# One K load of a decode attention kernel, cut into transfers of 112, 6, 6 and 4 partitions

## Chip, cores and metric

The kernel runs on one core of one Trainium2 chip. The metric is device time in microseconds (us) of one execution; lower is better. The times stated are medians over runs; beside them there is one profiled execution, from which the views are taken.

## The reference

A decode step for 4 sequences: layer norm, attention over a K/V cache of 32 heads and 4096 positions, a projection with a residual, then a layer norm and a small dense block with the mish activation and a second residual. Cut to what matters:

```python
# x (4,1,640), k_cache and v_cache (4,32,4096,128), wq (640,4096), wo (4096,640), all bf16
q = layernorm(x) @ wq                               # (4, 32 heads, 1, 128)
scores = einsum("bhqd,bhkd->bhqk", q, k_cache) * 128**-0.5
p = softmax(scores)
o = einsum("bhqk,bhkd->bhqd", p, v_cache)
h = x + o.reshape(4, 1, 4096) @ wo
y = layernorm(h) @ w1 + b1                          # w1 (640,1728)
act = y * tanh(softplus(y))
out = h + act @ w2                                  # w2 (1728,640)
```

Nearly all the bytes are the two caches: 4 x 32 x 4096 x 128 bf16 values each, 134 MB for K and 134 MB for V.

## The kernel before

**Groups.** The 4 x 32 pairs of sequence and head are worked in 32 groups (`NG = HQ * N`, 8 x 4). Group g belongs to one sequence b and G = 4 heads. Its K tile `kt` and its V tile `vt` have the shape [128, 128, 128]: 32 partitions to a head, 128 positions on each partition, 128 values to a position. So each partition holds 32 KB, which lie together in memory, and a load is 4 MB. `load_kv` (L88 to L97) issues it from the SP queue as one transfer of 128 partitions (L96). Only the last group's loads are made of two transfers, each of half the positions of all partitions (`np_`).

**Buffers and the order of loads.** There are two K buffers and two V buffers (`KBUFS`, `VBUFS`). The order is written out by hand in the loop over g: when group g's scores are done, K of group g+2 is issued into the buffer of group g; then V of group g+1. SP issues in this order, and before each it waits until the buffer's old content has been used: for K by VectorE and TensorE, for V by TensorE. The names K28, V27 and so on stand below for the loads of those groups. From K28 on the order is K28, V27, K29, V28, K30, V29, K31 (two transfers), V30, V31 (two), then w1, the rest of w2 (`w2s` of 128 and `w2r` of 64 partitions) and three parts of w2. Earlier loads are x (4 partitions, from the ACT queue), wq, four parts of wo and b1 (one partition).

**Work on a group.** `mul_and_sum` takes half a tile at a time (`part`): VectorE (DVE) multiplies K by the broadcast q in place (L337, two instructions to a part), and TensorE (PE) sums over d by matmuls with the identity (L344). `finish_sum` (L356) ends the sum on VectorE, `softmax` finds the maximum of each head through a transpose (L367 to L382) and takes the exponential on ScalarE (L387). `pv_moving` (L245) multiplies the weights by V for the group before; `add_blocks` (L259) folds its four blocks. The last two groups' products with V are taken by `pv` (L271) after the loop. Then come the projection (L318), the second layer norm, and the dense block (L514, L576), and one store of 20 partitions (L600).

On TensorE the order is that of the program: the sums of group g's second part stand before the V product of group g-1, and that before the sums of group g+1.

Of the kernel before, what the change touches and what calls it, by code (L numbers as in the profile page):

```python
# [16 lines left out]
def kernel(  # L17
# [23 lines left out]
    nc = tc.nc  # L41
# [4 lines left out]
    N = B * Sq  # L46
# [7 lines left out]
    HQ = H // G  # L54
# [4 lines left out]
    WOC = 8  # L59
    NQ = 2  # L60
    DQ = Dh // NQ
    KBUFS = 2
    VBUFS = 2
    NE2 = 2
# [12 lines left out]
    pad.tile([128, 192], BF16, name="pad")  # L77
    kpool = ctx.enter_context(tc.tile_pool(name="kpool", bufs=KBUFS))
    vpool = ctx.enter_context(tc.tile_pool(name="vpool", bufs=VBUFS))
# [8 lines left out]
    def load_kv(pool, tag, cache, g):  # L88
        hq, b = divmod(g, N)
        t = pool.tile([128, R, Dh], BF16, tag=tag, name=f"{tag}{g}")  # L90
        view = cache[b, G * hq : G * (hq + 1)].rearrange("h (p r) d -> (h p) r d", p=PH)

        np_ = NP if g == NG - 1 else 1
        for i in range(np_):
            r0, r1 = i * R // np_, (i + 1) * R // np_
            nc.sync.dma_start(out=t[:, r0:r1, :], in_=view[:, r0:r1, :])  # L96
        return t  # L97

    def load_k(g):
        return load_kv(kpool, "kt", A_k_cache, g)  # L100

    def load_v(g):
        return load_kv(vpool, "vt", A_v_cache, g)
# [35 lines left out]
    for q in range(G):  # L139
        nc.vector.tensor_copy(  # L140
            out=sel[:, :, q, q * PH : (q + 1) * PH],
            in_=ident[0:N, 0:N].unsqueeze(2).to_broadcast([N, N, PH]),
# [185 lines left out]
    def mul_and_sum(g, part):  # L328
# [6 lines left out]
        for k in range(NQ):  # L335
            d0 = k * DQ
            nc.vector.tensor_tensor(  # L337
                out=kt[:, :, d0 : d0 + DQ],
                in0=kt[:, :, d0 : d0 + DQ],
                in1=qbs[:, hq, b, d0 : d0 + DQ].unsqueeze(1).to_broadcast([128, RP, DQ]),  # L340
                op=ALU.mult,
            )
            for d in range(d0, d0 + DQ, W):
                nc.tensor.matmul(  # L344
# [52 lines left out]
    for g in range(NG):  # L397
# [31 lines left out]
        if g in WO_AT:  # L429

            if not wo_sb:
# [3 lines left out]
                out=wo_sb[0][:, h0 : h0 + WOC, :],  # L435
                in_=A_wo.rearrange("(h p) n -> p h n", p=128)[:, h0 : h0 + WOC, :],
# [60 lines left out]
    for dst in (h2T, hc):  # L497
        nc.vector.tensor_tensor(
            out=dst[:, :, :],
# [11 lines left out]
    for c in range(FC):  # L511
# [9 lines left out]
        if c == 4:  # L521
# [3 lines left out]
                out=std[:, :], in_=v_ps[:, :], func=ACT.Sqrt, bias=eps_t[:, :], scale=1.0  # L525
# [5 lines left out]
        out=h1n[:, :, :],  # L531
# [6 lines left out]
        out=h1s[:, :, :],  # L538
# [9 lines left out]
        out=tb[:, :, :],  # L548
# [8 lines left out]
        out=ta[:, :, :], in0=tb[:, :, :], scalar1=-0.5, scalar2=-1.0, op0=ALU.mult, op1=ALU.add  # L557
# [4 lines left out]
        out=act_t[:, :, :],  # L562
# [10 lines left out]
    for i, (w2, c) in enumerate(w2_of):  # L573
# [11 lines left out]
        out=oT[:, :, :].rearrange("p n c -> p c n"),  # L585
# [46 lines left out]
```

## Time and profile before

| what | value |
|---|---|
| time, median of 3 runs | 671.55 us (671.48 to 672.41) |
| time of the profiled execution | 672.24 us |
| its span (first to last instruction) | 670.4 us |
| PE busy | 562.8 us (84%) |
| DVE busy | 351.6 us (52%) |
| ACT busy | 112.2 us (17%) |
| DMA: bytes, mean rate over the span | 283.81 MB, 423 GB/s |
| queue q1 (all loads issued by SP): share of the 16 DMA engines' time | 98.6% |
| DVE's waits for K loads | 211.6 us in 30 waits |
| K load: issue to landing, median | 23.8 us |

The span is what the profile's views cover; what lies outside it (1.84 us here) is the difference to the profiled execution's time. The busy shares are means over the span. "Idle before, releaser" in a view is the time in which an engine stood still just before an instruction, and what ended it. A line `SPq` is SP's DMA queue; the time from issue to landing of a load contains its time in the queue behind the loads ahead of it. The profile's DMA line gives the busy share of all 16 DMA engines in tenths, in 40 slices of the span. Besides the views the trace holds a record of each DMA packet: start, duration, size and queue.

### The profile page before, as it was taken

What the parts mean: (1) busy time and instruction counts of PE and PEld (TensorE: products, weight loads), DVE (VectorE), ACT (ScalarE), POOL (GpSimd) and SP (SyncE); (2) the same over time, 40 slices, a digit from 0 to 9 for tenths busy, and PEclk for the clock granted to TensorE, in tenths of its full rate; (3) what the DMA queues carried; (4) which work ended last, traced back from release to release, by engine and by line L of the source; (5) the groups of instructions that cost most, each with busy time, mean ns of one, the idle gap of its engine ahead of it and who ended that gap; (6) DMA issues with size and microseconds to landing.
All of it is one profiled execution on the core that took longest, in us unless ns stands there. A gap on an engine that the chain in (4) does not pass through costs nothing.

```text
span 670.4 us, 7163 instructions
## 1 busy us (share of the span) xinstructions
PE 562.8 (84%) x3121; PEld 255.9 (38%) x3121; DVE 351.6 (52%) x304; ACT 112.2 (17%) x343; POOL 2.4 (0%) x13
## 2 busy tenths in 40 slices
PE   0589999799998886688998899869987899888985
PEld 0234444344443342233443344333433344333454
DVE  2385455455654456336664444666543566644642
ACT  0021121221220111011110111111101111110131
POOL 1000000000000000000000000000000000000000
PEclk9999999899997997878999899898999799997995
DMA  9999999999999999999999999999999999999994
GB/s 374 438 437 436 427 429 427 437 436 435 429 428 427 428 425 428 430 428 430 431 437 436 431 431 425 436 434 435 431 434 425 436 435 432 435 429 428 434 414 175
DMA packets 15191, 283.81 MB, mean 423 GB/s; under 512 B 1267, under 2 KB 5559, under 8 KB 6584
## 3 DMA queue, kind: packets, MB, share of 16 engines
q1 hardware_dynamic: 15152, 283.36, 98.6%
q8 instruction: 24, 0.39, 0.2%
q14 instruction: 7, 0.06, 0.0%
q10 hardware_dynamic: 8, 0.01, 0.0%
HBM read 283.35 MB, written 0.01 MB: 423 GB/s over the span
## 4 chain that ended last, share of the span: by engine, by line
PE 45%; DMA 34%; DVE 19%; issue 1%; ACT 1%; SPq 0%; DVEq 0%
DMA kt<-in_A_k_cache_dram 34%; PE s L344 21%; DVE kt L337 16%; PE p L245 15%; PE ot L259 3%; PE q_ps L191 1%; PE qb_ps L205 1%; PE ot L271 1%; PE tr L369 1%; DVE mx L374 1%; DVE s_sb L356 1%; ACT q_all L198 1%; PE l_ps L283 0%; PE h_ps L514 0%; PE yT L318 0%
## 5 line engine op out<-in xcount | busy, mean ns | idle before, releaser
L337 DVE TENSOR_TENSOR kt<-kt,qbs 128x4096 bf16<-128x4096 bf16 x128 | 291.4, 2279 | 211.6 <-DMA kt<-in_A_k_cache_dram 211.6
L344 PE MATMUL s<-kt,ident 128*128 128x512 bf16 x1024 | 262.9, 404 | 77.1 <-DVE kt L337 77.0
L245 PE MATMUL p<-vt,e 128*16 128x512 bf16 x960 | 215.8, 384 | 0.0
L344 PEld LDWEIGHTS <-ident 128*128 128x128 bf16 x1024 | 99.2, 102 | 197.5 <-issue 97.2
L245 PEld LDWEIGHTS <-e 128*16 128x16 bf16 x960 | 84.7, 91 | 131.0 <-issue 20.2
L387 ACT ACTIVATE e<-s_sb,nbs 32x128 bf16<-32x128 f32 x128 | 73.9, 577 | 2.5
L253 ACT COPY p_sb<-p 16x512 f32<-16x512 f32 x30 | 17.2, 574 | 317.9 <-PE p L245 317.9
L356 DVE TENSOR_REDUCE s_sb<-s 128x64 f32<-128x512 f32 x64 | 43.4, 679 | 3.8 <-PE s L344 3.7
L374 DVE TENSOR_REDUCE mx<-tr 1x4 f32<-1x128 f32 x32 | 8.9, 277 | 50.0 <-PE tr L369 49.8
L384 ACT COPY nbs<-tr 128x4 f32<-128x4 f32 x32 | 5.2, 162 | 173.0 <-PE tr L382 173.0
L259 PEld LDWEIGHTS ot<-ident_f,p_sb 16*128 16x128 f32 x240 | 28.9, 186 | 12.7 <-issue 12.7
L387 ACT ACTIVATION_READ_ACCUMULATOR e<-s_sb,nbs 32x1 f32 x128 | 32.1, 251 | 0.0
L259 PE MATMUL ot<-ident_f,p_sb 16*128 16x4 f32 x240 | 31.5, 250 | 0.0
L191 PE MATMUL q_ps<-wq_sb,xT 128*4 128x512 bf16 x40 | 11.0, 409 | 9.8 <-DMA wq_sb<-in_A_wq_dram 9.8
L382 PEld LDWEIGHTS tr<-mx,nscale 1*128 1x128 f32 x64 | 9.4, 183 | 13.8 <-issue 13.1
L291 DVE RECIPROCAL rl<-l_ps 128x16 f32<-128x16 f32 x8 | 2.1, 257 | 23.0 <-PE l_ps L283 23.0
L369 PE MATMUL tr<-ident_f,pm 128*1 128x128 f32 x64 | 12.9, 285 | 1.2 <-DVE pm L367 1.2
L205 PE MATMUL qb_ps<-q_all,sel 4*128 4x128 bf16 x128 | 9.2, 225 | 5.3 <-ACT q_all L198 5.3
L382 PE MATMUL tr<-mx,nscale 1*128 1x4 f32 x64 | 12.2, 258 | 0.4 <-DVE mx L374 0.4
L205 PEld LDWEIGHTS <-sel 4*128 4x128 bf16 x128 | 8.4, 98 | 9.1 <-issue 9.1
L198 ACT CAST q_all<-q_ps 4x512 bf16<-4x512 f32 x8 | 4.6, 574 | 35.4 <-PE q_ps L191 35.4
L367 DVE TENSOR_REDUCE pm<-s_sb 128x1 f32<-128x128 f32 x32 | 9.2, 286 | 1.1
(79 smaller groups left out, 75.1 us busy)
## 6 DMA issues: line engine op xcount, KB each, us to landing
kt<-in_A_k_cache_dram SPq DMA_DIRECT2D x31, 4096.0 KB, 23.8
vt<-in_A_v_cache_dram SPq DMA_DIRECT2D x31, 4096.0 KB, 26.5
wq_sb<-in_A_wq_dram SPq DMA_DIRECT2D x1, 5120.0 KB, 15.4
wo_sb<-in_A_wo_dram SPq DMA_DIRECT2D x4, 1280.0 KB, 29.0
kt<-in_A_k_cache_dram SPq DMA_DIRECT2D x2, 2048.0 KB, 19.0
vt<-in_A_v_cache_dram SPq DMA_DIRECT2D x2, 2048.0 KB
w<-in_B_w_dram SPq DMA_DIRECT2D x1, 2160.0 KB, 21.2
w<-in_B_w_dram SPq DMA_DIRECT2D x3, 640.0 KB, 19.5
```

Of the source, the lines that this page charges most:

```text
L191: nc.tensor.matmul(q_ps[:, :], lhsT=xT[:, c, :], rhs=wq_sb[:, c, n * QC : (n + 1) * QC], start=(c == 0), stop=(c == DC - 1),)
L205: nc.tensor.matmul(qb_ps[:, b * Dh : (b + 1) * Dh], lhsT=sel[:, b, q, :], rhs=q_all[:, h * Dh : (h + 1) * Dh], start=(q == 0), stop=(q == ...
L245: nc.tensor.matmul(p_ps[:, :], lhsT=e2[g % NE2][:, r : r + J, :].rearrange("p j q -> p (j q)"), rhs=vt[:, r : r + J, :].rearrange("p j d - ...
L253: nc.scalar.copy(out=blocks[g][:, :], in_=p_ps[:, :])
L259: nc.tensor.matmul(o, lhsT=p_sb[:, j * Dh : (j + 1) * Dh], rhs=ident_f[0 : J * G, j * G : (j + 1) * G], start=(j == 0), stop=(j == J - 1),)
L337: nc.vector.tensor_tensor(out=kt[:, :, d0 : d0 + DQ], in0=kt[:, :, d0 : d0 + DQ], in1=qbs[:, hq, b, d0 : d0 + DQ].unsqueeze(1).to_broadcas ...
L344: nc.tensor.matmul(s_ps[:, :, :], lhsT=ident[:, :], rhs=kt[:, :, d : d + W], start=(d == 0), stop=(d == Dh - W),)
L356: nc.vector.tensor_reduce(out=s_sbs[g][:, part * RP : (part + 1) * RP], in_=s_of.pop((g, part))[:, :, :], axis=AX.X, op=ALU.add,)
L369: nc.tensor.matmul(tr_ps[0:1, 0:128], lhsT=pm[:, :], rhs=ident_f[:, :], start=True, stop=True)
L374: nc.vector.tensor_reduce(out=mx[:, :], in_=tr_ps[0:1, 0:128].rearrange("o (a b) -> o a b", a=G), axis=AX.X, op=ALU.max,)
L382: nc.tensor.matmul(nb_ps, lhsT=nscale[:, :], rhs=mx[:, :], start=True, stop=True)
L387: nc.scalar.activation(out=e2[g % NE2][p0:p1, :, q], in_=s_sb[p0:p1, :], func=ACT.Exp, bias=nb[p0:p1, q : q + 1], scale=SCALE, accum_out=r ...
```

## The change

`load_kv` makes the K load of one group, number N * HQ - 4 = 28 of 0 to 31, out of four transfers instead of one: partitions 0 to 111, 112 to 117, 118 to 123, and 124 to 127. All four are issued in a row from the SP queue, at the place where the one was issued. The bytes, the tile and everything else are the same; every other load stays one transfer of 128 partitions.

```diff
     DQ = Dh // NQ
+    FEW = ("kt", N * HQ - 4)
     KBUFS = 2
...
         np_ = NP if g == NG - 1 else 1
+
+        cuts = (0, 112, 118, 124, 128) if (tag, g) == FEW else (0, 128)
         for i in range(np_):
             r0, r1 = i * R // np_, (i + 1) * R // np_
-            nc.sync.dma_start(out=t[:, r0:r1, :], in_=view[:, r0:r1, :])
+            for p0, p1 in zip(cuts, cuts[1:]):
+                nc.sync.dma_start(out=t[p0:p1, r0:r1, :], in_=view[p0:p1, r0:r1, :])
         return t
```

## The prediction

> **What bounds the kernel now.** I read the page first, slices and queues, then the waits, the chain of the last 110 us, the timelines of SP and DVE there, and last the packet records. The page says that the 16 DMA engines never rest:
>
> ```profile
> DMA  9999999999999999999999999999999999999994
> GB/s 374 438 437 436 427 429 427 437 436 435 429 428 427 428 425 428 430 428 430 431 437 436 431 431 425 436 434 435 431 434 425 436 435 432 435 429 428 434 414 175
> q1 hardware_dynamic: 15152, 283.36, 98.6%
> q8 instruction: 24, 0.39, 0.2%
> ```
>
> Queue q1 (the loads) fills 98.6% of the engines' time, at some 432 GB/s. Engines this busy leave one thing to gain or lose: how evenly work lies on them. The waits name who pays:
>
> ```profile
> DVE kt L337 <- DMA kt<-in_A_k_cache_dram: 211.6, 30, 19.3
> ```
>
> VectorE's multiply by q waits 30 times for a K load. In DVE's timeline the first multiplies of groups 28, 29 and 30 read:
>
> ```profile
> 574.91 2.29 DVE L337 TENSOR_TENSOR kt<-kt,qbs 128x4096 bf16<-128x4096 bf16 x1 [8.22 <-DMA kt<-in_A_k_cache_dram]
> 594.23 2.29 DVE L337 TENSOR_TENSOR kt<-kt,qbs 128x4096 bf16<-128x4096 bf16 x1 [8.72 <-DMA kt<-in_A_k_cache_dram]
> 613.89 2.29 DVE L337 TENSOR_TENSOR kt<-kt,qbs 128x4096 bf16<-128x4096 bf16 x1 [5.92 <-DMA kt<-in_A_k_cache_dram]
> ```
>
> And the chain that ended last:
>
> ```profile
> 568.68 25.53 DMA kt<-in_A_k_cache_dram
> 594.23 2.29 DVE kt L337
> ...
> 608.03 3.57 PE s L344 x8
> 611.60 7.91 PE p L245 x32
> 619.52 1.83 PE s L344 x8
> ```
>
> Its last DMA is the K load of group 29 (K29), issued at 568.68 and landed at 594.23. From there on it is DVE and PE up to the output. K30 lands at 613.89 while PE is busy with p until 619.52: not on the path. So whatever moves **the last byte of K29** moves the end one for one. The altered load, K28, is two loads ahead of it (K28, V27, K29).
>
> **The streams in the packet records.** The trace holds start, duration, size and queue of each packet, not its engine. Where one packet's start meets another's end, they can be chained, and the loads form 16 streams without gaps: eight packets of 32 KB, 1.213 us each, and a semaphore packet per 4 MB load, so 9.68 us a load. 32 KB in 1.213 us is 27.0 GB/s, times 16 is the 432 of the page. (These records run 10.8 us ahead of the engines' clock: K29's last packet ends at 605.07, DVE starts at 594.23.) What sets streams apart is q8: eight of them carry its 24 packets (0.88 to 1.19 us) in turn; each costs its stream some 1.4 us, which it never wins back. At K29 the eight stand 2.85, 2.92, 3.05, 3.20, 3.21, 4.34, 4.37 and 4.51 us behind the earliest stream; the other eight 0, 0.13, 0.39, 0.44, 0.75, 1.06, 1.21, 1.54. K29 waits for the 4.51.
>
> **The change, part by part.**
>
> Issue: three more transfers on SP at 551.77. Two in a row took 0.80 (K31), so 3 x 0.40 = 1.2 us. The SP timeline shows them covered:
>
> ```profile
> 551.77 0.33 SPq L96 DMA_DIRECT2D kt<-in_A_k_cache_dram  x1
> 558.77 0.33 SPq L96 DMA_DIRECT2D vt<-in_A_v_cache_dram  x1
> 568.68 0.33 SPq L96 DMA_DIRECT2D kt<-in_A_k_cache_dram  x1
> ```
>
> V27 is issued 7.0 us later, after a wait for PE, and its packets start some 11 us after that. Cost 0; if that cover were gone, 1.2 us on V27, which lands at 584.6, 2.8 us before PE's p for it begins (587.4). DVE waits for four semaphores where it waited for one, and 3 x 9 ns of semaphore packets are added. K30's issue also names them, but it waits for K28 to be used up anyway: 0.
>
> Which stream gets which rows: in this trace 128 rows go eight to a stream, w2r's 64 rows four, the output's 20 rows as two packets each with ten semaphore packets, x's 4 rows as four, b1's one row as one. The count of streams is the largest up to 16 that divides the rows. So 112 becomes seven rows on all 16, and 6, 6, 4 become one row on six, six and four streams. Whether they begin at the same stream, the trace cannot say; I take it that they do. Then four streams have 10 rows, two have 9, ten have 7.
>
> In stream time alone: 7 rows instead of 8 are -1.21 us, 10 are +2.42. If late streams are among the ten, the 4.51 becomes 3.30. Two signs say so: b1's single row went down the stream at 0.44, and a row of x that took 755 ns ended 3 ns ahead of wq's first row on the stream now at 1.06. Both are among the eight without q8. The latter, as one of the four, becomes 1.06 + 2.42 = 3.48, and the worst of its kind 1.54 + 2.42 = 3.96. K29 would move by -1.03 to -0.55.
>
> The other half is **where the 16 rows land**. In a full load each stream writes eight partitions of its own, so the trace does not tell whether 27.0 GB/s is what a stream gives or what its partitions take. The 16 rows all go to partitions 112 to 127, and up to six streams write next to each other at once. Bounds: below, no sharing, one row per transfer, 3 x 1.21 = 3.63 us for streams 2 and 3 of the six. Above, all 16 rows through one 27.0 GB/s door, 16 x 1.21 = 19.4 us. Between: doors of four partitions. Then 112-115, 120-123 and 124-127 each pass four rows of different streams, 4 x 1.21 = 4.84 us, and streams 2 and 3 are in all three: 14.5 us. The nearest rows are w2r's, 64 partitions from 16 streams: 55 ns for 1280 bytes in 44 of 64 packets, up to 84 in the rest, where w2s (128 partitions, same size) stays at 55 in 117 of 128. That is contention, up to 84/55, in a burst of only 5 KB per stream; for 32 KB rows it says little. I take the doors of four, the least sharing in which 27.0 GB/s belongs to partitions, since a rate that is the same to 1 ns in 7881 of 7936 packets looks like a fixed door and not a shared memory.
>
> The Trainium skill's page "SBUF — State Buffer", section "Door 1: The DMA port swizzle", speaks against the change: 16 ports of about 27 GB/s each serve two groups of four partitions, and a transfer to four partitions is put at 27.6 GB/s in all, one to 64 at 196. By that page 112-115, 116-119, 120-123 and 124-127 are four ports, shared with the streams already writing V27 there; my estimate by it is +9 us. No row here shows 32 KB writes to one group.
>
> Sum: streams 2 and 3 need 7 x 1.21 + 14.5 = 23.0 us for K28 where they needed 9.68: +13.3. They start between 0 and 1.54 where the last stood at 4.51, so K29's last byte moves by 13.3 - 4.51 + (0 to 1.54) = +8.8 to +10.3. I take +8.8, as streams that finish early leave the door to others. K28 itself is later by as much: its 8.22 us of waiting grows, its 10.6 us of work (574.91 to 585.51 on DVE) still ends before K29 lands. Against the profiled execution (span 670.4, time 672.24, so 1.84 outside the span) that is 681.0; against the median of the runs, 671.55, which is 0.69 lower, **680.4**.
>
> **Rivals.**
>
> No shared door, early streams take the rows: K29 moves by -0.55 to -1.03, at most one row, -1.21. Time 670.3 to 671.0, say 670.8. For it: streams never disturb each other in 32 KB rows, and both signs on b1 and x. Against: they never had to share partitions. It decides if four streams into four partitions pass 32 KB in under 1.6 us each: 7 x 1.21 + 3 x 1.6 is 13.3, plus 1.06, just above 9.68 + 4.51. This is the case that ends not slower; by 0.18% at most, so hardly over the bound of 0.2% (1.34 us), about what a measurement of this kernel can tell from no change.
>
> No shared door, but the rows fall on streams with q8: 2.85 + 2.42 to 4.51 + 2.42, so +0.8 to +2.4, time 672.3 to 674.0. Against it the two signs above.
>
> The change does not load any stream more: the small transfers begin on streams in rotation, or each row is cut over all 16. Each stream has eight rows as before: 671.5, if there is no door; +3.6 (4.84 - 1.21) if there is.
>
> A door half as tight (two streams' worth) belongs to the forecast's own side: 8.47 + 3 x 2.42 + 1.06 - 14.2 = +2.6, 674.1. The widest sharing gives 13.3 + 4.9 - 4.51 + (0 to 1.54) = +13.7 to +15.2, 685 to 687.
>
> **How the numbers follow.** Shared door 0.68; no door and early streams 0.20; no door and late streams 0.06; no load shifted 0.06. Slower by over 0.2%: 0.68 + 0.05 of the late streams + 0.01 = 0.74. Faster by over 0.2% needs the whole row and some luck: 0.08 (a cause unseen included). The rest, 0.18, is within. The second case has 0.20, so the range reaches down to it, 670.3; up to 684.0, which leaves out the widest sharing, about 0.1. The forecast's own range is 674.1 to 687.
>
> **What would show it.** Right: the 128-row K packets keep 1.213 us, but the 16 packets of the small transfers take 4 us or more; DVE's wait ahead of group 28 grows from 8.22 to about 17 us and that ahead of 29 stays near 8.7; K29's landing moves from 594.2 to about 603; the chain behind it keeps its 74 us. Wrong: the small packets take 1.21 us (no door), DVE starts on group 29 before 594.2, or the 16 packets lie on 16 streams.

## The result, and the profile after

The change takes **688.23 us** (median of 5 runs, 687.93 to 689.42) against 671.55 of the kernel before on the same chip: a ratio of 1.0247, 95% interval 1.0235 to 1.026, or +16.7 us. The forecast was 680.4 with a range of 670.3 to 684.0. The direction held and the size did not: the loss is nearly twice the +8.8 us that were worked out. The profiled execution after has a span of 686.4 us, 16.0 more than before.

The page of the profile after, first the DMA rows (busy tenths and GB/s in 40 slices of 17.16 us) and the shares of two queues:

```profile
DMA  9999999999999999999999999999999999999994
GB/s 382 441 427 428 427 434 442 432 429 430 431 429 436 428 421 432 417 438 438 431 429 431 427 435 436 435 429 432 429 436 437 432 368 201 315 434 432 437 408 184
q1 hardware_dynamic: 15168, 283.36, 98.7%
q8 instruction: 24, 0.39, 0.2%
```

The busy row is the one of before, nines throughout, and q1's share is still 98.7%. The GB/s row is not: three neighbouring slices read 368, 201 and 315 where 432 is the normal pace. Against 432 they miss 64 + 231 + 117 = 412 GB/s for 17.16 us, 7.07 MB, and at 432 GB/s that is 16.4 us. The whole loss stands in these three numbers. The engines read as busy all the while, with transfers that went at less than their pace.

The waits, and the first multiplies of groups 28, 29 and 30 in VectorE's timeline (start, duration, operation, idle time before it and what ended it; L341 is the L337 of before):

```profile
DVE kt L341 <- DMA kt<-in_A_k_cache_dram: 223.1, 30, 25.7
```

```profile
591.86 2.29 DVE L341 TENSOR_TENSOR kt<-kt,qbs 128x4096 bf16<-128x4096 bf16 x1 [25.73 <-DMA kt<-in_A_k_cache_dram]
610.85 2.29 DVE L341 TENSOR_TENSOR kt<-kt,qbs 128x4096 bf16<-128x4096 bf16 x1 [7.76 <-DMA kt<-in_A_k_cache_dram]
630.17 2.29 DVE L341 TENSOR_TENSOR kt<-kt,qbs 128x4096 bf16<-128x4096 bf16 x1 [5.58 <-DMA kt<-in_A_k_cache_dram]
```

K28's wait went from 8.22 to 25.73 us, those of K29 and K30 hardly moved (8.72 to 7.76, 5.92 to 5.58). K28 is ready 16.95 us later than before, K29 16.62 us later. The loss arises while K28 is under way and is passed on, with nothing added or won back. The chain that ended last goes over K29 as before:

```profile
568.11 42.71 DMA kt<-in_A_k_cache_dram
610.85 2.29 DVE kt L341
...
653.27 22.56 DMA w<-in_B_w_dram
```

K29 is issued at 568.11, 0.6 us earlier than before, and takes 42.71 us instead of 25.53. Behind it the chain now passes over w1's load, but is no longer for it: 686.4 - 610.85 = 75.6 us, where before it was 76.2. SP's timeline shows what the additional issues cost:

```profile
551.20 1.37 SPq L100 DMA_DIRECT2D kt<-in_A_k_cache_dram  x4
558.21 0.35 SPq L100 DMA_DIRECT2D vt<-in_A_v_cache_dram  x1
568.11 0.35 SPq L100 DMA_DIRECT2D kt<-in_A_k_cache_dram  x1
```

Four issues take 1.37 us and are over 5.6 us before V27's.

**The packet records.** The normal 32-KB row takes 1.213 us. The records (on their clock, which runs 10.8 us ahead of the engines') hold 26 32-KB rows over 1.3 us before, each beside a packet of an instruction queue (q8 or q14), and 216 after. 191 of these stand in one stretch, from 571 to 603. Chained into 16 streams, as in the prediction, they divide so:

| rows | how long each took (us) | time over 1.21 us a row, summed, divided by 16 streams |
|---|---|---|
| 21 rows of V26, ahead | up to 2.53 | 1.3 us |
| the 112-partition transfer, seven rows on each of 16 streams | median 2.40 | 9.0 us |
| the 16 rows of the three small transfers | 2.6 to 3.7, medians 3.10, 3.29, 3.38 | 2.0 us |
| 42 rows of V27, behind | up to 3.66 | 3.9 us |
| sum | | 16.2 us, beside a span longer by 16.0 us |

All 16 streams are slow, not the four or six that carry small rows, and rows of the neighbouring whole loads are slow with them.

### The profile page after: what moved, and what is told of

It is laid out like the page before. It is cut to its first block, busy times and chain, and to the rows that moved or that the text cites. A ratio compares the mean times of both kernels' runs of the same rounds, so it can differ in the third digit from the quotient of the medians.

```text
span 686.4 us, 7172 instructions
## 1 busy us (share of the span) xinstructions
PE 563.1 (82%) x3121; PEld 256.2 (37%) x3121; DVE 351.5 (51%) x304; ACT 112.2 (16%) x343; POOL 2.4 (0%) x13
## 3 DMA queue, kind: packets, MB, share of 16 engines
q1 hardware_dynamic: 15168, 283.36, 98.7%
## 4 chain that ended last, share of the span: by engine, by line
PE 42%; DMA 39%; DVE 17%; ACT 1%; issue 1%; SPq 0%; DVEq 0%
DMA kt<-in_A_k_cache_dram 36%; PE s L348 20%; DVE kt L341 15%; PE p L249 15%; DMA w<-in_B_w_dram 3%; PE ot L263 3%; PE q_ps L195 1%; PE qb_ps L209 1%; PE tr L373 1%; DVE mx L378 1%; DVE s_sb L360 1%; ACT q_all L202 1%; PE h_ps L518 0%; PE l_ps L287 0%; PE y2T L580 0%
## 5 line engine op out<-in xcount | busy, mean ns | idle before, releaser
L341 DVE TENSOR_TENSOR kt<-kt,qbs 128x4096 bf16<-128x4096 bf16 x128 | 291.5, 2279 | 223.1 <-DMA kt<-in_A_k_cache_dram 223.1
L257 ACT COPY p_sb<-p 16x512 f32<-16x512 f32 x30 | 17.2, 574 | 320.0 <-PE p L249 320.0
L386 PEld LDWEIGHTS tr<-mx,nscale 1*128 1x128 f32 x64 | 9.4, 183 | 13.8 <-issue 13.1
```

The lines of the kernel that those rows point to most:

```text
L257: nc.scalar.copy(out=blocks[g][:, :], in_=p_ps[:, :])
L341: nc.vector.tensor_tensor(out=kt[:, :, d0 : d0 + DQ], in0=kt[:, :, d0 : d0 + DQ], in1=qbs[:, hq, b, d0 : d0 + DQ].unsqueeze(1).to_broadcas ...
L386: nc.tensor.matmul(nb_ps, lhsT=nscale[:, :], rhs=mx[:, :], start=True, stop=True)
```

## The experiments

Three theories stand in the expectations. A "door" in them is whatever passes the writes of the DMA engines into a group of neighbouring partitions; it is a name for a guess, and no record shows one. **A**: streams that write to partitions behind a common door share its pace, and this slows all 16 streams. **B**, the prediction's: only the streams that carry rows into a shared door are slowed, the rest runs on. **C**: it is the reading side, the addresses that a cut load reads, and the partitions have no part in it. Ratios are to the kernel before in runs of the same chip; the spans are those of one profiled execution each (before: 670.4).

### Only one cut: 112 and 16 partitions

```diff
-        cuts = (0, 112, 118, 124, 128) if (tag, g) == FEW else (0, 128)
+        cuts = (0, 112, 128) if (tag, g) == FEW else (0, 128)
```

> K28 in two transfers, of 112 and of 16 partitions: seven rows and then one row on each of the 16 streams, so no stream carries more bytes than before. Known from the run of the change: during the 112 every row on every stream took about 2.4 us instead of 1.21. Theory A (streams that write neighbouring partitions share a door, and all 16 streams go at the pace of the fullest door): 7 x 1.2 = +8.4 us for the 112, and 16 rows into four groups of four partitions, 4 x 1.21 = 4.84 instead of 1.21, +3.6; about 683.5 us. Theory B (as predicted: only the streams in the small transfers are slowed): +3.6, 675.2. Theory C (the reading side: seven rows read one after another by each stream are the trouble, not the partitions): +8.4 for the 112 and nothing for the 16, 680.

Measured: 687.81 us, ratio 1.0246 (1.0219 to 1.0274), as long as the change. Here no stream carries more rows than before: seven of one transfer and one of the other. So the uneven tail of 6, 6 and 4, on which the prediction spent its working, costs nothing that these runs can tell; one cut at 112 costs it all. B is out, and C's and A's numbers are both too low; what A priced too low is seen below.

### Even cuts: 64 and 64, then four times 32

```diff
-        cuts = (0, 112, 118, 124, 128) if (tag, g) == FEW else (0, 128)
+        cuts = (0, 64, 128) if (tag, g) == FEW else (0, 128)
```

> K28 in two transfers of 64 partitions, four rows on each of the 16 streams in each. Theory A and B alike: the eight doors of 64 partitions serve 16 streams, two to a door, so each row takes 2.42 us: 8 x 1.21 = +9.7, 681.2 us. Theory C: each stream reads four rows that lie together, less than the seven of the 112; if seven cost 1.2 us a row, four cost less: 671.5 to 676. No theory puts more bytes on any stream.

```diff
+        cuts = (0, 32, 64, 96, 128) if (tag, g) == FEW else (0, 128)
```

> K28 in four transfers of 32 partitions, two rows on each of the 16 streams in each. If a door is eight adjacent partitions, 32 of them have four doors for 16 streams: 4.84 us a row, 8 x 3.63 = +29 and more, above 700 us. If a door is four adjacent partitions and the four 32 further on, 32 have eight doors, as many as 64: rows of 2.4 to 2.5 us as in the run of two transfers of 64, and its time, 686 us.

Measured: 686.05 us, ratio 1.0214 (1.0199 to 1.0229), and 685.9 us, ratio 1.021 (1.0196 to 1.0224). Both lose the same, though in one a transfer spreads over 64 partitions and in the other over 32. The windows (window, length, busy us of PE, PEld, DVE, ACT and POOL with counts, granted clock, DMA's busy share, GB/s) show the same pace, first for the kernel before, then for 64 and 64, then for four times 32:

```profile
562.00:574.00 12.00, 11.58 (x58) 5.38 (x57) 4.70 (x3) 2.48 (x9) 0.00 (x0) 1.00 1.00 430
```

```profile
562.00:574.00 12.00, 11.06 (x55) 5.20 (x54) 5.07 (x4) 2.48 (x9) 0.00 (x0) 1.00 1.02 218
```

```profile
562.00:574.00 12.00, 10.46 (x52) 5.00 (x51) 4.29 (x3) 2.47 (x9) 0.00 (x0) 1.00 1.02 218
```

The last two columns are the reading: a busy share of 1.02, and 218 GB/s, half of the 430 of before. Most slow rows took 2.2 to 2.6 us in both, about twice 1.213. Two streams meet at each door, as it seems, whether 64 or 32 partitions are offered.

The Trainium skill's page "SBUF — State Buffer", section "Door 1: The DMA port swizzle", says that partitions 0 to 31 reach as many ports as 0 to 63, since four adjacent partitions and the four that lie 32 further on have one port; it puts 32 and 64 partitions at 189 and 196 GB/s for transfers of 1 MiB, and both at about 218 as the limit for large ones. The 218 of these two windows agrees with the equality and with the limit.

The forecast of A for the first of them, 681.2, doubles K28's 128 rows, 8 x 1.21 = 9.7 us on each stream. The measured loss is 14.6 us. Rows of V26 ahead and of V27 behind are slow too, and K28's ran a little over the double.

### Sixteen transfers of eight partitions, four apart

```diff
+            if (tag, g) == FEW:
+                for j in range(16):
+                    s0 = 32 * (j // 4) + j % 4
+                    nc.sync.dma_start(out=t[s0 : s0 + 29 : 4, r0:r1, :], in_=view[s0 : s0 + 29 : 4, r0:r1, :])
+                continue
```

> K28 in 16 transfers of 8 partitions, four partitions apart (0, 4, .. 28; 1, 5, .. 29; and so on; then from 32, 64 and 96). Eight streams carry 16 rows, the other eight none. Theory C or no door: 8 rows more on these, +9.7, less the 4.5 - 3.0 us by which the latest of them stood ahead of the latest stream: +8.1, 679.7; all rows 1.21 us. Theory A or B: the eight partitions of one transfer are in eight doors, so the eight rows of partitions 0 to 63 take 1.21 us each; those of 64 to 127 meet the other eight streams, which write there for the next load: 2.42 us, so 8 x 1.21 more: +17.8, 689.3. By A all 16 streams are slowed in that second half and none in the first.

Measured: 687.08 us, ratio 1.0231 (1.0212 to 1.025), near the number of A and B, but not by their road. Eight rows use eight streams, and the issues alone hold SP, so that V27 starts only behind them:

```profile
550.47 25.09 SPq L102 DMA_DIRECT2D kt<-in_A_k_cache_dram  x16
576.21 0.34 SPq L105 DMA_DIRECT2D vt<-in_A_v_cache_dram  x1
```

Two windows, the first with K28 alone on eight streams, the second with V27 beside it:

```profile
566.00:570.00 4.00, 4.00 (x20) 1.74 (x20) 0.19 (x1) 0.00 (x0) 0.00 (x0) 1.00 0.47 201
578.00:590.00 12.00, 0.00 (x0) 0.00 (x0) 0.00 (x0) 0.00 (x0) 0.00 (x0) 0.55 0.97 210
```

Half the engines move 201 GB/s, all of them 210. In the records, with eight packets in flight (575 to 588 on their clock), the rows take 1.213 us (the longest of them 1.28), three quarters of the 16 transfers. From 588 on, a microsecond after V27's issue in that clock, 16 are in flight, and most rows take 2.2 to 2.6 us until K28 is through at about 603. The cut load reads in the same manner in both stretches; what changes is that V27's streams run beside K28's. So the cuts themselves are not slow, nor the rows that they read by themselves. That V27's streams write at the places at which K28's are at work fits this, but no record tells which partitions a stream writes.

### The reading side alone

```diff
+            if (tag, g) == FEW:
+                rows = cache.rearrange("b h (p r) d -> (b h p) r d", p=PH)
+                nc.sync.dma_start(out=t[:, r0:r1, :], in_=rows[0 : 7 * 127 + 1 : 7, r0:r1, :])
+                continue
```

> K28 in one transfer of 128 partitions as before, but its rows are read from every seventh row of the K cache (so group 28 works on other rows; the amount of work is the same). Only the addresses read change. Theories A and B: nothing changes, 671.5 us, rows of 1.21 us. Theory C: the rows of K28 take longer, up to 2.4 us: 672 to 681.

Measured: 671.69 us, ratio 1.0002 (0.9992 to 1.0012). VectorE starts on group 28 where it did before (574.91):

```profile
574.94 2.29 DVE L345 TENSOR_TENSOR kt<-kt,qbs 128x4096 bf16<-128x4096 bf16 x1 [8.83 <-DMA kt<-in_A_k_cache_dram]
```

Other addresses, apart from each other, with the same 128 partitions written: nothing. C falls in the form that could be tried here. In every other run the rows that a transfer reads go with the partitions that it writes, so the two sides were not taken apart any further.

### One door beside a whole load, and its control

K28 is left whole here. Behind it four small transfers of four rows of 8 KB go to a tile that nothing reads: to adjacent partitions in the first kernel, to partitions four apart in the second.

```diff
+        if (tag, g) == FEW:
+            for p0, p1, st in ((80, 84, 1), (112, 116, 1), (84, 88, 1), (116, 120, 1)):
+                nc.sync.dma_start(
+                    out=spare[p0:p1:st, :].rearrange("p (r d) -> p r d", d=Dh),
+                    in_=view[p0:p1:st, 0:32, :],
+                )
```

> K28 whole again (128 partitions). Behind it four more transfers of four adjacent partitions each (80-83, 112-115, 84-87, 116-119), rows of 8 KB, into a part of SBUF that is free by then; 128 KB more in all, which nothing reads. Alone a row of 8 KB is 0.30 us. Theory B (only the streams that share are slowed): four streams and the owner of the door get a fifth each, 1.5 us a row, 6 us on four early streams; K29 later by at most 6 + 1.85 - 4.55 = 3.3 us, 674.8 us or less, and of the other twelve streams only two at a time have rows of over 1.3 us (some 4 to 8 rows of 32 KB in all). Theory A (all streams go at the pace of the fullest door): rows of over 1.3 us on all 16 streams for some 6 us, 40 or more, mean shift +3 us or more, 675 to 678. No door at all: 0, 671.5.

```diff
+            for p0, p1, st in ((32, 45, 4), (33, 46, 4), (34, 47, 4), (35, 48, 4)):
```

> The control to the run before: the same four transfers of four rows of 8 KB, the same count of streams and bytes, but the partitions of each are four apart (32, 36, 40, 44; 33, ..), so that each of the four streams writes where it writes in a full load. Theories A and B: no door is shared; 4 x 0.30 = 1.2 us on four early streams, which stand 2.7 us or more ahead of the latest: 671.5 us, within 0.2%, no slow rows. If small transfers cost by themselves (their number, their few streams), it is as slow as the run before.

Measured: 674.13 us, ratio 1.0034 (1.0024 to 1.0045), with adjacent partitions; 672.29 us, ratio 1.0003 (0.9993 to 1.0012), in the control. So 128 KB more cost 2.3 us or nothing, and neither their number nor their few streams is the reason. What differs is where they land, and with it which rows of K28's share they are read from: adjacent rows in the first, rows four apart in the control. The windows of the first, before and within:

```profile
566.00:570.00 4.00, 4.00 (x21) 1.84 (x22) 0.32 (x1) 0.00 (x0) 0.00 (x0) 1.00 0.97 418
571.00:575.00 4.00, 4.00 (x20) 1.62 (x18) 0.00 (x0) 0.00 (x0) 0.00 (x0) 1.00 0.92 236
```

and the second window in the control:

```profile
571.00:575.00 4.00, 4.00 (x21) 1.62 (x19) 0.00 (x0) 0.00 (x0) 0.00 (x0) 1.00 0.97 416
```

236 against 416 GB/s, for 4 us. Only four streams carry small rows, yet in the records every 32-KB row that started between 582 and 584, 16 rows, took 1.77 us or more. By B the others would have stayed at 1.21. The time alone does not decide here between A and B: 674.13 is within B's bound of 674.8 and below A's 675 to 678. The records do. B expected some 4 to 8 slow rows on the twelve streams without small rows, A 40 or more on all 16; there are 31 more than before in all. And if, as B's expectation counts, four streams and two others at a time were held up, ten would keep their 27 GB/s, 270 in all by this estimate; the window shows 236. So a crowded door slows streams that have nothing to bring there. Why it does is not shown by any record.

The Trainium skill's page "DMA: Bandwidth & Descriptors", section "Back-pressure in remote DMA", says of transfers from SBUF to SBUF of another core that a saturated port at the destination clogs the way back to the source engines and to others that share that way. The 236 beside 416 is what such clogging would look like, in loads from HBM, which the section does not speak of.

### Eight transfers of 16

```diff
+        cuts = (0, 16, 32, 48, 64, 80, 96, 112, 128) if (tag, g) == FEW else (0, 128)
```

> K28 in eight transfers of 16 partitions, one row on each of the 16 streams in each; no stream carries more bytes. Cuts that leave two streams to a door (64, 32) made rows of 2.4 to 2.5 us and cost 14.5 us. Here 16 adjacent partitions have four doors, so four streams to a door. If all streams go at the pace of the fullest door: rows of 4.8 us, 8 x 3.63 = +29, and as the loads behind are slowed too (14.5 measured where 9.7 were worked out) up to +44: 700 to 715 us. If any sharing just halves the rate: rows of 2.4 us, 686 us.

Measured: 692.06 us (689.04 to 697.75), ratio 1.0338 (1.0291 to 1.0386), a profiled span of 687.2. More is lost than with 32 or 64 partitions, as A has it, but the pace is far from a quarter: most slow rows take 2.3 to 3.4 us, not 4.8. The window that read 218 GB/s above reads 175 here:

```profile
562.00:574.00 12.00, 9.35 (x47) 4.53 (x46) 4.05 (x3) 2.48 (x9) 0.00 (x0) 1.00 1.00 175
```

The profiled execution, 689.04 us, is the shortest of the four, so its records show less than the median's loss. A's rule, that all streams go at the pace of the fullest door, overstates how far they slow. It may be that streams drift apart so that not all of a transfer stand at one door; this was argued, not tried.

### A version without the cut by partitions

The chain says that K29's last byte sets the end. K29 and K30 are therefore loaded, from the kernel before, as K31 is: in two transfers of half the positions of all 128 partitions.

```diff
-        np_ = NP if g == NG - 1 else 1
+        np_ = NP if g == NG - 1 or (tag == "kt" and g >= NG - 3) else 1
```

> From the kernel before, not the changed one: K29 and K30 are made, as K31 is, of two transfers of half the positions, all with 128 partitions (rows of 16 KB, 0.607 us, so 9.71 us a load instead of 9.68). If K29's last byte sets the end, its first half lands 4.8 us earlier and VectorE starts on it then; the first two multiplications (4.5 us) no longer wait for the last byte. The gain is bounded by what is next: w1's last byte lands 1.6 us before it is needed. So -1.0 to -1.6 us, 669.9 to 670.5. If the end is not set there, 0.

Measured: 670.65 us, ratio 0.9982 (0.9973 to 0.9991), 1.2 us faster than before on the same chip and within the forecast. VectorE begins with half of group 29 at 589.74 instead of 594.23:

```profile
589.74 2.29 DVE L337 TENSOR_TENSOR kt<-kt,qbs 128x4096 bf16<-128x4096 bf16 x1 [3.90 <-DMA kt<-in_A_k_cache_dram]
```

Of the 4.5 us only 1.2 arrive at the end. The chain of this kernel shows what is late next:

```profile
607.89 20.58 DMA kt<-in_A_k_cache_dram
628.50 2.29 DVE kt L337
...
633.71 24.65 DMA w<-in_B_w_dram
658.41 0.97 PE h_ps L514 x25
```

K29 is off it; now K31 and, behind it, w1's load stand there. And it is a split too: halves of the positions keep 128 partitions in each transfer, and cost no pace.

### The account over the runs

The time of 32-KB rows over 1.213 us, summed and divided by 16 streams, and the count of rows over 1.3 us, both less those of the kernel before (0.8 us, 26 rows), beside the growth of the profiled span over 670.4 us:

| K28's transfers | ratio | more slow rows | excess / 16 (us) | span (us) |
|---|---|---|---|---|
| 112, 6, 6, 4 (the change) | 1.0247 | 190 | 16.1 | +16.0 |
| 112, 16 | 1.0246 | 193 | 14.9 | +14.4 |
| 64, 64 | 1.0214 | 182 | 12.9 | +13.5 |
| four of 32 | 1.021 | 193 | 12.9 | +13.8 |
| eight of 16 | 1.0338 | 188 | 17.2 | +16.8 |
| sixteen of 8, four apart | 1.0231 | 94 | 6.8 | +16.3 |
| 128 and four small, adjacent | 1.0034 | 31 | 1.6 | +2.9 |
| 128 and four small, four apart | 1.0003 | 0 | 0.0 | +0.1 |
| 128, other rows of the cache | 1.0002 | 0 | 0.0 | +0.4 |

For the first five the slow rows account for the longer span to within 0.9 us. In the run of sixteen transfers eight streams also stood without a row from 574 to 588, which is 7.3 us over 16 streams. In the run with 128 KB more, the 8-KB rows, which this sum leaves out, took 0.31 to 1.07 us each.

## Why the prediction was wrong, step by step

- **K29's last byte moves the end one for one.** Right. K29 ready +16.62, span +16.0; the chain behind it 75.6 us instead of 76.2 (the prediction's 74 us ends at the issue of the output's store, 668.37).
- **Three more issues cost nothing.** Right: 1.37 us for four, covered.
- **Which stream gets which rows.** Right as far as the records tell: seven rows of the large transfer on each of 16 streams, and single rows of the small ones on six, six and four streams that begin at the same one. Four streams have three of them, two have two, and b1's stream is one of the four. "Late streams are among the ten" held for seven of the eight with q8.
- **The door.** That the place of landing matters, and that 27.0 GB/s does not belong to the stream alone, was right: with no stream loaded more, as with 112 and 16 or with 64 and 64, rows still took about 2.4 us, and small rows cost 2.3 us or nothing by their place. So the rival without a shared door is out, and so is the rival in which the small transfers lie on 16 streams, by the blocks of single rows. That the sign came out right owes something to luck all the same: single rows on a few streams, the forecast's term, are not needed for the loss (64 and 64 has none and lost 14.6 us).
- **The step that failed: "7 rows instead of 8 are -1.21 us", and with it the 7 x 1.21 in "7 x 1.21 + 14.5 = 23.0".** The large transfer was priced as if it were seven eighths of a whole load. Its rows took a median of 2.40 us, on every stream, 16.1 to 20.2 us for seven rows instead of 8.47. The run of 112 and 16 shows the whole loss without the uneven tail, and that of 64 and 64 most of it with no small transfer at all. The sum had the slowdown only in the 16 small rows, on two streams: 14.5 us for three rows. Those rows measured 2.6 to 3.7 us each, about 9 to 10 us for three. So the term that was worked out with care was too large, and the term that was taken for granted was short by 9.0 us in the mean of the 16 streams.
- **That a slow stream leaves the others alone.** Wrong, and of the same origin. The prediction set the loss off against the lateness of q8's streams (13.3 - 4.51). When all streams slow down, nothing is there to set off. It also held that 128-row packets keep 1.213 us; 21 rows of V26 and 42 of V27 did not, and account for 1.3 + 3.9 of the 16.2 us.
- **The signposts.** DVE's wait ahead of group 28 was to be 17 us and is 25.73; ahead of 29 it was to be 8.7 and is 7.76; K29's landing was to be 603 and is 610.85. The waits have the predicted pattern, with the size off. The packets do not: the small rows were to take 4 us or more and took 2.6 to 3.7, and rows of 128-row transfers were to keep 1.213 us.
- **The range.** Its upper end, 684.0, came from bounds on the small transfers alone, and even the widest sharing (685 to 687) stays below 688.23. No bound was put on the large transfer, though the trace of before shows no 112-row transfer either.

## What to carry to other kernels

On a kernel that its DMA engines bound, cut a load along the free dimension, not along partitions: halves of the positions cost nothing here, while halves of the partitions took a load from 1.21 to about 2.4 us a row, and its neighbours with it. If one part of a transfer has no example in the trace, every part of it needs a bound, also the large one that looks like the old transfer made a little smaller. Read GB/s beside the busy share of the DMA engines: the busy share read 1.0 at 218 GB/s as it did at 430.

## What the runs showed of the hardware that was not expected

- Rows to a common place slow streams that bring nothing there: 236 GB/s for 4 us with 16 rows of 8 KB to adjacent partitions, 416 with partitions four apart.
- Eight streams alone move 201 GB/s at 1.213 us a row, and 16 streams that meet one another 175 to 218, mostly at 2.2 to 3.4 us: half of the engines do about as much.
- Sixteen issues of one load held SP for 25.09 us, 1.6 us each, and eight (the transfers of 16 partitions) for 20.16 us, while four took 1.37 us, 0.34 each; what SP stood for in between was not looked into.
- What stays open: why a crowded door slows streams that write elsewhere, why four streams to a door (as A counts them) give 2.3 to 3.4 us and not 4.8, whether the rows read have a part in it beyond the one form tried, and which partitions a stream of a 112-row transfer writes at a time, which no record holds.
